# A second staging buffer and fewer GpSimd steps in a list-scheduled transformer block

## The chip, the cores and the metric

The kernel runs on one core of a Trainium2 chip. The metric is device time in microseconds (us) of one execution, lower is better. Before the change it took 759.53 us (median of three runs, 758.91 to 760.48); in the rounds that compare it with the changed kernel, 760.0 us (median of four, 758.91 to 761.48).

Short names, as the profile uses them: PE is TensorE, DVE is VectorE, ACT is ScalarE, POOL is GpSimd, SP is SyncE. L534 means line 534 of that kernel's source. An edit that adds lines shifts the numbers: L534 of before is L536 of after.

## The reference

One block with adaptive layernorm: linear attention, then a GEGLU feed-forward network.

```python
# S = 2048 rows, D = 1024, F = 3584, 32 heads; inputs bfloat16
mod = (silu(c) @ w_mod).reshape(..., 6, 1, -1)        # sa, ca, ga, sb, cb, gb
h = layernorm(x) * (1 + ca) + sa
x = x + ga * linear_attention(h, wqkv, wo)
h = layernorm(x) * (1 + cb) + sb                      # the second norm
x = x + gb * ((gelu(h @ w_gate) * (h @ w_up)) @ w_down)
```

## The kernel before

The kernel runs in stages: key/value/query, W_o, then twice (for two halves of the rows, g = 0 and 1) gate/up and down. Many matrix products use seven block products in place of eight, nested in places to a second level, so DVE makes many sums of blocks. Two jobs for later run behind the first gate/up stage:

- `wd_sums` makes second-level sums of W_down in seven steps: load rows, add on DVE, copy the result (768 KB) through a staging buffer `u` out to DRAM;
- `late_norm` normalises the second half's rows, in eight tiles.

```python
wdu_ring = Ring(199, [3, 4, HB], F16, 1)      # ONE staging buffer, 6 KB per partition

def wd_sums(c):
    raw, t, u, tt = wdr_ring(), wdt_ring(), wdu_ring(), wds_ring()
    # ... two loads (raw rows, first-level sums), ten sums on DVE into u and tt ...
    def last():
        tt_op(*steps[-1], ALU.add)
        gp.dma_start(out=u_scr[:, c], in_=u)                    # "us<-mem" in the profile
        for j in range(2):
            gp.dma_start(out=wd_full[f"t{2 * j + 1}"][:, rows, :], in_=tt[:, j])

def tile_norm(tl):                                              # in late_norm, cut
    sy.dma_start(out=xt, in_=x2_scr[b][r:r + P, :])
    ac.activation(out=junk, in_=xt, func=AF.Copy, accum_out=nmean)             # L1135
    gp.tensor_scalar(out=nmean, in0=nmean, scalar1=-1.0 / D, scalar2=None, op0=ALU.mult)  # L1136
    ac.activation(out=junk, in_=xt, func=AF.Square, bias=nmean, accum_out=ssq) # L1137
    gp.tensor_scalar(out=rstd, in0=ssq, scalar1=1.0 / D, scalar2=1e-5, op0=ALU.mult, op1=ALU.add)
    gp.tensor_tensor(out=rstd, in0=rstd, in1=nhalf, op=ALU.pow)
    gp.tensor_tensor(out=nb, in0=nmean, in1=rstd, op=ALU.mult)
    ac.activation(out=xh, in_=xt, func=AF.Identity, scale=rstd, bias=nb)
    gp.dma_start(out=xh_scr[g][b % 2][r:r + P, :], in_=xh)
```

Operations are not issued in the order written. The kernel has its own list scheduler: every call is recorded as an op with the memory it touches and a cost. PE's order is fixed; forward and backward sweeps decide the order on the other engines, and the best order by the model is issued. The cost model thus touches no data but moves instructions everywhere:

```python
elif op.eng == "POOL":
    op.cost = op.lat = 700 + n / 0.5          # ns; n = elements per partition
# ...
DMA_LATENCY, GBPS = 1500, 360                 # assumed: a DMA lands 1.5 us after its bytes at 360 GB/s

def issue(self):
    for op in self.order():                   # list schedule from op.cost, op.lat, dependencies
        self.calls[op.line](getattr(self.engines[op.eng], op.fn), op.args, op.kw)
```

These costs are what the scheduler assumes, not measurements.

Lines to know in the profile of before: L534 is the helper of all block sums on DVE; L781 copies a product from PSUM on ACT; L1284 and L1295 are first- and second-level matmuls of gate/up; L1338 is ACT seeding an accumulator; L1487 and L1531 are the down stage's matmuls.

Of the kernel before, what the change touches and what calls it, by code (L numbers as in the profile page):

```python
# [11 lines left out]
BF16 = mybir.dt.bfloat16  # L12
F16 = mybir.dt.float16
AF = mybir.ActivationFunctionType
ALU = mybir.AluOpType
# [8 lines left out]
class Plan:  # L24
# [98 lines left out]
    def cost(self, op, outs, ins):  # L123

        size = lambda a: math.prod(d[1] for d in a.ap[1:])
        n = max(size(a) for a in (outs if op.eng == "PE" else outs + ins))
        psum = any(a.tensor.name.startswith("psum") for a in outs + ins)
        wide = any(a.dtype == FP32 and size(a) > 8 for a in outs + ins)
        ptrs = sum(size(a) == 1 for a in ins)
        if op.eng == "PE":  # L130
            op.cost = n / 2.4 + 2.5
            op.lat = op.cost + 165
            if op.fn == "matmul" and outs[0].ap[0][1] <= 32:
                op.cost /= 3.5
        elif op.fn.startswith("dma"):
            a = outs[0]
            op.cost, op.bytes = 1000 if op.eng == "POOL" else 450, math.prod(d[1] for d in a.ap) * (4 if a.dtype == FP32 else 2)
            op.bytes *= 2 if "accum_op" in op.kw else 1
            op.load = a.tensor.name.startswith("mem")
            if op.fn == "dma_start_transpose":  # L140
                op.cost, op.bytes = self.transpose
            op.lat = op.cost
        elif op.eng == "ACT":
            op.cost = (55 if psum else 112) + n / 1.2 + 85 * ptrs
            op.lat = op.cost + 115
            f = op.kw.get("func")
            op.table = "g" if f == AF.Gelu_apprx_tanh else "e" if f in (AF.Exp, AF.Ln) else None
        elif op.eng == "POOL":
            op.cost = op.lat = 700 + n / 0.5
        else:  # L150
            rate = 1.0
            if op.fn in ("tensor_scalar", "tensor_scalar_mul", "tensor_scalar_add", "tensor_copy") and not wide:
                rate = 1.0 if psum else 4.0
            elif op.fn == "tensor_tensor" and not wide:
                rate = 2.0
            op.cost = 69 + n / (0.96 * rate) + 61 * ptrs
            op.lat = op.cost + 83
# [119 lines left out]
def kernel(  # L277
# [19 lines left out]
    S, D = x_in.shape  # L297
# [77 lines left out]
    def at(off, shape, dt):  # L375
        return Ring(off, shape, dt, 1)()
# [43 lines left out]
    HB = TG // 2  # L420
# [36 lines left out]
    rstd_ring = Ring(206.625, [1], FP32, 8)  # L457
    nb_ring = Ring(206.75, [1], FP32, 8)
    sum_ring = Ring(206.25, [1], FP32, 8)
# [25 lines left out]
    wds_ring = Ring(193, [2, 2, NW], F16, 1)  # L485
    wdt_ring = Ring(197, [2, NW], F16, 1)
    wdu_ring = Ring(199, [3, 4, HB], F16, 1)
    sub_a = [at(76 + 3.5 * j, [NPR // 2, HB], F16) for j in range(3)]
    sub_b = [at(189 + 3.5 * j, [NPR // 2, HB], F16) for j in range(4)]
    x2_ring = Ring(191, [D], BF16, 4)  # L490
    x2e_ring = Ring(144, [D], BF16, 3)
    xhe_ring = Ring(150, [D], F16, 3)
    junk = at(156, [D], F16)
    xh2_ring = Ring(199, [D], F16, 3)

    psT = Banks(0, 3)
# [23 lines left out]
    te, ve, ac, gp, sy = (plan.on(e) for e in ("PE", "DVE", "ACT", "POOL", "SP"))  # L520
# [605 lines left out]
    def late_norm(g):  # L1126


        def tile_norm(tl):
            b, r = 2 * g + tl // TT, tl % TT * P  # L1130
            xt, xh = x2e_ring(), xhe_ring()
            sy.dma_start(out=xt, in_=x2_scr[b][r:r + P, :])
            load = plan.ops[-1]
            nmean, ssq, rstd, nb = sum_ring(), sum_ring(), rstd_ring(), nb_ring()
            ac.activation(out=junk, in_=xt, func=AF.Copy, accum_out=nmean)  # L1135
            gp.tensor_scalar(out=nmean, in0=nmean, scalar1=-1.0 / D, scalar2=None, op0=ALU.mult)  # L1136
            ac.activation(out=junk, in_=xt, func=AF.Square, bias=nmean, accum_out=ssq)  # L1137
            gp.tensor_scalar(out=rstd, in0=ssq, scalar1=1.0 / D, scalar2=1e-5, op0=ALU.mult, op1=ALU.add)
            gp.tensor_tensor(out=rstd, in0=rstd, in1=nhalf, op=ALU.pow)
            gp.tensor_tensor(out=nb, in0=nmean, in1=rstd, op=ALU.mult)  # L1140
            ac.activation(out=xh, in_=xt, func=AF.Identity, scale=rstd, bias=nb)
            gp.dma_start(out=xh_scr[g][b % 2][r:r + P, :], in_=xh)
            return load

        return [lambda tl=tl: tile_norm(tl) for tl in range(2 * TT)]
# [573 lines left out]
```

## Time and profile before

| what | before |
|---|---|
| median of runs | 760.0 us |
| span of the profiled run | 757.8 us |
| busy: PE / DVE / ACT / POOL | 97% / 82% / 54% / 14% |
| granted TensorE clock | 1.0 |
| first gate/up stage (first matmul to first down matmul) | 173.8 us |
| second gate/up stage | 165.5 us |

The page of before: busy time of each engine, then PE's busy tenths and the granted clock, also in tenths, in 40 slices of the span.

```profile
span 757.8 us, 11401 instructions
## 1 busy us (share of the span) xinstructions
PE 735.8 (97%) x4164; PEld 391.6 (52%) x4164; DVE 622.7 (82%) x1288; ACT 412.2 (54%) x697; POOL 105.2 (14%) x199
...
PE   5999999999999999989999999999999999999997
...
PEclk9999999999999999999999999999999999999999
```

PE is full nearly everywhere (97% busy), so only a change that shortens PE's waits can win. How much is there? In the timeline, 40 matmuls of 512 columns start from 253.07 to 261.70 us: 0.216 us each. The first gate/up stage has 680 of these and 182 of 256 columns at 0.108 us, an estimate of 166.3 us; it takes 173.8, so it loses about 7.5 us.

PE's timeline of before in that stage, only lines with a wait of some size: start, length, engine, line, operation, operands, count, and in brackets PE's idle time ahead of it with its releaser.

```profile
326.22 1.02 PE L1284 MATMUL psum<-mem 128*128 128x512 f16 x4 [0.58 <-DVE mem L534]
327.75 0.38 PE L1295 MATMUL psum<-mem 128*128 128x256 f16 x2 [0.51 <-DVE psum L534]
331.62 0.38 PE L1295 MATMUL psum<-mem 128*128 128x256 f16 x2 [0.68 <-DVE psum L534]
338.61 1.02 PE L1284 MATMUL psum<-mem 128*128 128x512 f16 x4 [1.00 <-ACT mem L781]
377.13 1.02 PE L1284 MATMUL psum<-mem 128*128 128x512 f16 x4 [0.25 <-DVE mem L534]
378.67 0.38 PE L1295 MATMUL psum<-mem 128*128 128x256 f16 x2 [0.51 <-DVE psum L534]
382.13 0.38 PE L1295 MATMUL psum<-mem 128*128 128x256 f16 x2 [0.28 <-DVE psum L534]
```

There are three clusters: 326 to 332, 338.6, and 377 to 382 us. These gaps sum to less than the 7.5 us, because the view counts from a modelled end of the matmul before, about 0.16 us late (a 512-column matmul of L1284 lasts 379 ns in the page and the next starts after 216); smaller delays don't appear.

DVE's waits in the same stage (us in total, times, the longest), the DMA line of it:

```profile
DVE mem L534 <- DMA us<-mem: 4.9, 2, 3.0
```

DVE waited twice for a copy-out of its staging buffer. The chain of waits of before leads from the first one to PE (start, length, what):

```profile
310.91 8.86 DMA us<-mem
319.77 0.02 issue
319.79 2.37 DVE mem L534 x8
...
331.62 0.38 PE psum L1295 x2
...
335.17 1.65 POOL mem L1136
336.81 0.02 issue
336.84 1.24 ACT mem L1137 x2
338.08 0.49 ACT mem L781
338.57 0.04 issue
338.61 1.02 PE psum L1284 x4
```

A copy-out issued at 310.91 us lands 8.86 us later, and only then may the next step's sums fill the buffer; the first two gaps and the third follow from DVE being late. Then ACT stands between two passes of a late-norm tile for GpSimd's negate (L1136), which took 1.65 us here, and the copy that PE needs stands behind it in ACT's queue. Five of before's eight negates took 221 to 252 ns. What ran beside this one (the timeline of all engines from 333.6 to 336.9 us, two of its lines):

```profile
333.29 3.43 DVE L534 TENSOR_TENSOR mem<-mem 128x512 f16<-128x512 bf16 x10
335.17 1.64 POOL L1136 TENSOR_SCALAR mem<-mem 128x1 f32<-128x1 f32 x1
```

It ends (at 336.81 us) when a run of DVE sums with both operands in SBUF ends (336.72). The three long negates of before (1637, 1030 and 442 ns) lie beside such sums for 1550, 932 and 358 ns of their time, the five short ones for at most 84 ns. That is what the trace shows side by side.

The third cluster follows the other DVE wait, 1.9 us at 374 us: there the down stage's own sums overwrite the staging buffer, and the last copy-out is still under way.

### The profile page before, as it was taken

The numbers are of one execution on the slowest core, as the hardware profiler recorded it, in microseconds if no ns is written. First come the engines' busy times: TensorE is split into PE (matmuls) and PEld (weight loads), VectorE is DVE, ScalarE is ACT, GpSimd is POOL, SyncE is SP. The second block draws the span as 40 slices with busy tenths as digits, with TensorE's granted clock in tenths as the row PEclk, the third lists the DMA queues.
The fourth block names the chain that finished last, engine by engine and source line by source line (L and its number), as shares of the span: only waits on it lengthen the run. The fifth ranks groups of instructions, "written<-read, shape, count | busy, mean of one in ns | idle before, by whom it ended". The sixth has DMA issues, their size and how long they took to land.

```text
span 757.8 us, 11401 instructions
## 1 busy us (share of the span) xinstructions
PE 735.8 (97%) x4164; PEld 391.6 (52%) x4164; DVE 622.7 (82%) x1288; ACT 412.2 (54%) x697; POOL 105.2 (14%) x199
## 2 busy tenths in 40 slices
PE   5999999999999999989999999999999999999997
PEld 2454545443444445444445486645555555548664
DVE  7898986589897899899877779578889899897763
ACT  3674676668766578767565234016666666621000
POOL 1331433007121123141000001010000000000000
PEclk9999999999999999999999999999999999999999
DMA  9847067879389578875432999852323313399822
GB/s 313 304 119 253 27 154 165 299 286 178 100 242 312 210 263 289 281 261 211 135 103 52 290 275 280 290 185 84 112 65 102 112 56 112 101 273 294 281 100 74
DMA packets 140759, 144.78 MB, mean 191 GB/s; under 512 B 33440, under 2 KB 120864, under 8 KB 139936
## 3 DMA queue, kind: packets, MB, share of 16 engines
q1 hardware_dynamic: 124016, 106.31, 46.0%
q0 software_dynamic: 14336, 35.66, 15.1%
q10 hardware_dynamic: 2352, 2.10, 0.8%
q8 instruction: 32, 0.52, 0.3%
q14 instruction: 23, 0.19, 0.1%
HBM read 111.81 MB, written 32.24 MB: 190 GB/s over the span
## 4 chain that ended last, share of the span: by engine, by line
PE 76%; DVE 7%; ACT 5%; DMA 5%; issue 4%; POOL 1%; SPq 1%; POOLq 0%; DVEq 0%; ACTq 0%
PE psum L1284 25%; PE psum L1487 13%; PE psum L1531 8%; PE psum L836 6%; PE psum L1295 6%; PE psum L1176 6%; DVE mem L534 5%; PE psum L906 4%; PE psum L935 4%; DMA us<-mem 2%; DMA mem<-in_A_wqkv_dram 2%; DMA mem<-in_w_mod_dram 1%; PE psum L950 1%; PE psum L962 1%; DVE mem L975 1%
## 5 line engine op out<-in xcount | busy, mean ns | idle before, releaser
L534 DVE TENSOR_TENSOR mem<-mem 128x512 f16<-128x512 f16 (+11 forms) x633 | 292.0, 506 | 15.1 <-DMA us<-mem 4.9
L1284 PE MATMUL psum<-mem 128*128 128x512 f16 x1248 | 299.3, 379 | 2.8 <-ACT mem L781 1.0
L534 DVE TENSOR_TENSOR mem<-psum,mem 128x512 f16<-128x512 f32 (+4 forms) x260 | 192.3, 748 | 70.7 <-ACT mem L781 25.8
L781 ACT ACTIVATE mem<-psum 128x256 f32<-128x256 f32 (+2 forms) x228 | 123.2, 554 | 119.2 <-PE psum L1284 43.2
L1284 PEld LDWEIGHTS <-mem 128*128 128x128 f16 (+1 forms) x1248 | 122.1, 98 | 114.4 <-issue 5.2
L1487 PE MATMUL psum<-mem 128*128 128x512 f16 (+2 forms) x462 | 99.2, 373 | 0.5 <-DVE mem L534 0.5
L1295 PE MATMUL psum<-mem 128*128 128x256 f16 x560 | 89.5, 272 | 2.4 <-DVE psum L534 2.2
L1295 PEld LDWEIGHTS <-mem 128*128 128x128 f16 (+1 forms) x560 | 54.7, 98 | 48.1 <-issue 6.5
L1487 PEld LDWEIGHTS <-mem 128*128 128x128 f16 x462 | 45.2, 98 | 49.9 <-issue 0.7
L1338 ACT ACTIVATE psum<-psum 128x512 f32<-128x512 f32 x56 | 32.9, 587 | 62.1 <-PE psum L1284 31.5
L1531 PE MATMUL psum<-mem 128*128 128x256 f16 (+1 forms) x588 | 66.2, 273 | 0.0
L836 PE MATMUL psum<-mem 128*128 128x512 f16 (+1 forms) x280 | 62.5, 379 | 0.0
L1531 PEld LDWEIGHTS <-mem 128*128 128x128 f16 x588 | 57.5, 98 | 9.2
L1176 PE MATMUL psum<-mem 128*128 128x512 f16 x256 | 57.4, 379 | 0.7 <-DVE mem L534 0.7
L906 PE MATMUL psum<-mem 128*128 128x512 f16 x224 | 51.1, 379 | 0.1
L534 DVE TENSOR_TENSOR psum<-psum,mem 128x256 f32<-128x256 f32 x80 | 34.1, 426 | 11.5 <-ACT mem L781 11.5
L836 PEld LDWEIGHTS <-mem 128*128 128x128 f16 x280 | 27.0, 98 | 31.2
L1355 ACT ACTIVATE mem<-psum 128x512 f16<-128x512 f32 x56 | 33.3, 596 | 17.4 <-PE psum L1284 17.1
L1176 PEld LDWEIGHTS <-mem 128*128 128x128 bf16 x256 | 25.1, 98 | 31.0 <-issue 0.9
L906 PEld LDWEIGHTS <-mem 128*128 128x128 f16 (+1 forms) x224 | 21.4, 97 | 26.9 <-issue 2.1
L1365 ACT ACTIVATE mem<-mem 128x512 f16<-128x512 f16 x56 | 34.9, 629 | 0.5 <-DVE mem L534 0.3
L612 DVE BATCH_NORM_STATS2 mem<-mem 128x6 f32<-128x512 bf16 x48 | 30.9, 677 | 1.5 <-DMA mem<-in_A_x_dram 1.5
(127 smaller groups left out, 564.8 us busy)
## 6 DMA issues: line engine op xcount, KB each, us to landing
mem<-in_B_w_gate_dram SPq DMA_DIRECT2D x14, 1024.0 KB, 5.2
mem<-in_B_w_up_dram SPq DMA_DIRECT2D x14, 1024.0 KB, 5.7
mem<-in_w_mod_dram SPq DMA_DIRECT2D x24, 512.0 KB, 6.7
mem<-us SPq DMA_DIRECT2D x24, 448.0 KB, 7.8
mem<-in_A_x_dram SPq DMA_DIRECT2D x32, 256.0 KB, 3.9
ts<-in_B_w_down_dram POOLq DMA_DIRECT2D x28, 256.0 KB, 7.2
us<-mem POOLq DMA_DIRECT2D x7, 768.0 KB, 7.4
mem<-in_B_w_down_dram SPq DMA_DIRECT2D x12, 448.0 KB, 7.1
```

Of the source, the lines that this page charges most:

```text
L534: ve.tensor_tensor(out=out, in0=a, in1=b, op=op)
L781: ac.activation(out=t, in_=ps, func=AF.Copy)
L836: te.matmul(ps, lhsT=A[:, k, i * P:(i + 1) * P], rhs=B[:, k, :], start=(start and k == 0), stop=(k == KH - 1), skip_group_check=True)
L906: te.matmul(o, lhsT=W[:, k, (j0 + i) * P:(j0 + i + 1) * P], rhs=h_form(a, k), start=(start and k == 0), stop=(k == KH - 1), skip_group_che ...
L1176: te.matmul(psw[:, half, :], lhsT=pqT[b][:, g, tl * P:(tl + 1) * P], rhs=Wp[:, g, half * NW:(half + 1) * NW], start=(g == 0), stop=(g == K ...
L1284: te.matmul(ps, lhsT=a[:, k, e, :], rhs=b[:, k, :], start=(start and k == 0), stop=(k == KH - 1), skip_group_check=True)
L1295: te.matmul(ps, lhsT=self.x[a][:, k, :], rhs=self.y[y][:, k, :], start=(start and k == 0), stop=(k == KH // 2 - 1), skip_group_check=True)
L1338: ac.activation(out=z, in_=x, func=AF.Copy)
L1355: ac.activation(out=o, in_=ps, func=AF.Gelu_apprx_tanh)
L1365: ac.activation(out=o, in_=o, func=AF.Gelu_apprx_tanh)
L1487: te.matmul(psm[:, q, c], lhsT=A[:, i, q * P:(q + 1) * P], rhs=wt[:, i, c], start=(start and i == 0), stop=(i == NPR - 1), skip_group_chec ...
L1531: te.matmul(ps[:, q, :], lhsT=a[:, k, q * P:(q + 1) * P], rhs=y[:, k, :], start=(start and q == 0 and k == 0), stop=(k == NPR // 2 - 1), s ...
```

## The change

The intent: the late norm gives most of its 128x1 operations to DVE and loses one (the negate folds into a scale on the ACT pass); the staging buffer gets a twin; and the scheduler is told that a small GpSimd operation costs less time but a longer latency. The diff is complete:

```diff
         elif op.eng == "POOL":
-            op.cost = op.lat = 700 + n / 0.5
+            op.cost = 500 if n <= 8 else 250 + n / 0.46
+            op.lat = 1800 if n <= 8 else op.cost
@@
     wdu_ring = Ring(199, [3, 4, HB], F16, 1)
+    wdu_ring.slots += Ring(183, [3, 4, HB], F16, 1).slots
@@
-    junk = at(156, [D], F16)
+    junk = at(156, [D], BF16)
@@
-            nmean, ssq, rstd, nb = sum_ring(), sum_ring(), rstd_ring(), nb_ring()
-            ac.activation(out=junk, in_=xt, func=AF.Copy, accum_out=nmean)
-            gp.tensor_scalar(out=nmean, in0=nmean, scalar1=-1.0 / D, scalar2=None, op0=ALU.mult)
-            ac.activation(out=junk, in_=xt, func=AF.Square, bias=nmean, accum_out=ssq)
-            gp.tensor_scalar(out=rstd, in0=ssq, scalar1=1.0 / D, scalar2=1e-5, op0=ALU.mult, op1=ALU.add)
+            nmean, var, rstd, nb = sum_ring(), sum_ring(), rstd_ring(), nb_ring()
+            root = D ** -0.5
+            ac.activation(out=junk, in_=xt, func=AF.Copy, scale=-root / D, accum_out=nmean)
+            ac.activation(out=junk, in_=xt, func=AF.Square, scale=root, bias=nmean, accum_out=var)
+            ve.tensor_scalar_add(out=rstd, in0=var, scalar1=1e-5)
             gp.tensor_tensor(out=rstd, in0=rstd, in1=nhalf, op=ALU.pow)
-            gp.tensor_tensor(out=nb, in0=nmean, in1=rstd, op=ALU.mult)
+            ve.tensor_scalar(out=nb, in0=nmean, scalar1=rstd, scalar2=1.0 / root, op0=ALU.mult, op1=ALU.mult)
             ac.activation(out=xh, in_=xt, func=AF.Identity, scale=rstd, bias=nb)
```

So the change has three named parts, called here cost, slot and norm, and a fourth thing that none of its lines says: the order that the scheduler makes from them. A comparison of the two instruction streams shows PE's order the same, and other orders on DVE, ACT, POOL and SP.

## The prediction

> **What bounds the kernel.** The page of before: PE is busy 97% of a 757.8 us span, DVE 82%, ACT 54%, POOL 14%; granted clock 1.0. Gaps in the PE timeline: about 8.7 us at the start, some 3.5 us from 174 to 239 us, and 4.5 us in the first gate/up stage (253 to 427 us). That stage lasts 174 us; its 680 matmuls of 512 columns at 0.216 us and 182 of 256 columns at 0.108 us need about 166 us (estimate from the trace's pitch), so it loses nearly 8 us; the second gate/up stage loses about 2.
>
> In the first stage DVE is nearly full (5.8 to 6.0 us of most 6 us slices). The chain of waits shows two places where it is late: the copy-out of the W_down second-level sums, issued at 310.9 us, lands at 319.8 us, and DVE idles 2.97 us for its single buffer; PE then loses 0.58, 0.51 and 0.68 us. A later copy-out (issued 365.75, landed 374.3) costs DVE 1.9 us and PE about 1.0 us. A third loss, 1.00 us at 338.6 us, goes through the late norm: ACT waits 1.27 us for POOL's negate, which took 1.64 us instead of its usual 0.22 us.
>
> **What the change does.** Matmul order is identical. (1) The Copy-to-Square round trip through POOL is gone (0.53 us mean plus handoff, per tile). Sixteen 128x1 operations are new on DVE: one of 128x8 takes 0.157 us, some 0.1 us of pitch, so 1.6 to 2.6 us of DVE work, where DVE is full. POOL had time for its 8 us. [...]
> (2) The second staging buffer removes the wait at 316.8 us: reuse is then two sums (about 25 us) away, against 8.9 us to land. The 374 us wait stays: there the down stage's sums overwrite the first buffer, and the new order keeps about the same distance (some 13 DVE operations).
> (3) The scheduler's new GpSimd cost reorders DVE, ACT and POOL, in the first 180 us too, where PE has hardly a gap: nothing to win, a little to lose.
>
> **Sum.** Won: 1.8 us (staging wait) + 1.0 us (POOL round trip) + up to 1 us of small seed waits; with less behind it, perhaps 2 more. Given back: 1 to 2 us by added DVE work and by DVE[...] now itself waiting for ACT's sums and POOL's power (three late tiles are bunched, and the down stage's differences wait for their last ACT passes). Net -2 to -4 us.
>
> Predicted 756.5 us; 8 times in 10 within 752.5 to 760. Chances: faster by over 2% 0.01, within 2% 0.97, slower 0.02.
>
> **What would show it.** The 2.97 us DVE wait near 317 us is gone, and PE's gaps at 326 to 332 us with it; the one near 374 us remains; ACT no longer waits for POOL before Square; the first gate/up stage is 2 to 4 us shorter than 174 us, the others equal within 1 us; sixteen DVE operations of 0.15 us appear.
>
> **What would make it wrong.** DVE blocked on POOL's power behind DMA issues, or on ACT in the bunched tail, for several us; other single buffers (raw rows, first-level sums, their copy-outs) taking over the wait; the reordered first third opening PE gaps; or all of the loss freed, up to 6 us.

The sum: its net of -2 to -4 us on the 759.53 us of before gives 755.5 to 757.5, and 756.5 is the middle.

## The result, and the profile after

The changed kernel is correct and takes 756.72 us (median of four runs, 755.78 to 758.08) against 760.0 us: a ratio of 0.9957, 95% interval 0.9933 to 0.9981. A ratio here is the mean time of one kernel's fast runs over that of the other's of the same rounds, so not quite the ratio of the medians.

Stage by stage, from the first matmul of each stage in the profiled runs:

| stage | before | after | difference |
|---|---|---|---|
| up to W_o (keys, values, queries) | 192.3 | 192.9 | +0.6 |
| W_o | 60.8 | 60.8 | 0.0 |
| first gate/up | 173.8 | 171.0 | -2.9 |
| first down | 80.4 | 80.4 | 0.0 |
| second gate/up | 165.5 | 164.9 | -0.6 |
| second down, end | 85.0 | 85.0 | 0.0 |

The same lines of the page of after (without the heading):

```profile
span 754.9 us, 11379 instructions
PE 734.4 (97%) x4144; PEld 391.3 (52%) x4164; DVE 623.4 (83%) x1304; ACT 411.6 (55%) x697; POOL 95.8 (13%) x175
```

Twenty-four small operations left POOL (199 to 175) and sixteen came to DVE (1288 to 1304); the other eight are gone. (PE's 4144 for 4164 is matmul records missing from the trace, since the weight loads are 4164 in both.)

All of PE's waits in the first gate/up stage of after:

```profile
294.79 4.48 PE L1286 MATMUL psum<-mem 128*128 128x512 f16 x20 [0.33 <-ACT psum L1340]
312.29 1.02 PE L1286 MATMUL psum<-mem 128*128 128x512 f16 x4 [0.21 <-ACT mem L783]
319.95 4.48 PE L1286 MATMUL psum<-mem 128*128 128x512 f16 x20 [0.19 <-ACT psum L1340]
```

All three clusters are gone in this profile, the one near 377 too, which the prediction expected to stay. DVE's waits in the stage, all lines of 1 us or more but those on PE and on the copies of L783:

```profile
DVE mem L1140 <- ACT mem L1139: 2.5, 2, 1.5
...
DVE mem L536 <- DMA mem<-ts: 2.0, 1, 2.0
...
DVE mem L536 <- DMA mem<-in_B_w_down_dram: 1.0, 1, 1.0
```

No wait for `us<-mem` is left. In its place DVE now waits 3.0 us for two loads of the sums' inputs, and 2.5 us for ACT's Square pass ahead of the new epsilon addition (L1140). None of these reaches PE as a gap of more than 0.33 us in this profile. The sixteen new DVE operations, by line (duration min/median/max in ns):

```profile
L1140 DVE TENSOR_SCALAR mem<-mem x8: 143/151/154, 267.0 to 347.9; 128x1 f32<-128x1 f32 x8
```

```profile
L1142 DVE TENSOR_SCALAR mem<-mem x8: 203/206/208, 268.6 to 368.5; 128x1 f32<-128x1 f32 x8
```

They are 8 x 0.151 + 8 x 0.206 = 2.9 us of DVE time. Where DVE has nothing to wait for, the next operation starts 0.06 to 0.20 us after the start of one of them ("some 0.1 us of pitch" in the prediction). The addition, L1140, has an immediate operand; L1142 multiplies by a [128, 1] operand and an immediate.

Nothing here yet says which part did what, since order, slot, norm and cost changed at once.

### The profile page after: what moved, and what is told of

Its sections match the earlier page's. It is cut to its first block, busy times and chain, and to the rows that moved or that the text cites. A ratio compares the mean times of both kernels' runs of the same rounds, so it can differ in the third digit from the quotient of the medians.

```text
span 754.9 us, 11379 instructions
## 1 busy us (share of the span) xinstructions
PE 734.4 (97%) x4144; PEld 391.3 (52%) x4164; DVE 623.4 (83%) x1304; ACT 411.6 (55%) x697; POOL 95.8 (13%) x175
## 4 chain that ended last, share of the span: by engine, by line
PE 80%; DVE 8%; ACT 6%; DMA 4%; issue 1%; SPq 1%; DVEq 0%; ACTq 0%
PE psum L1286 28%; PE psum L1489 13%; PE psum L1533 9%; PE psum L1297 7%; DVE mem L536 7%; PE psum L838 6%; PE psum L1178 6%; PE psum L908 4%; PE psum L937 4%; DMA mem<-in_A_wqkv_dram 2%; DMA mem<-in_B_w_up_dram 1%; DMA mem<-in_w_mod_dram 1%; PE psum L952 1%; ACT psum L965 1%; ACT mem L967 1%
## 5 line engine op out<-in xcount | busy, mean ns | idle before, releaser
L536 DVE TENSOR_TENSOR mem<-psum,mem 128x512 f16<-128x512 f32 (+4 forms) x260 | 192.3, 748 | 67.5 <-ACT mem L783 22.6
L783 ACT ACTIVATE mem<-psum 128x256 f32<-128x256 f32 (+2 forms) x228 | 123.2, 555 | 121.1 <-PE psum L1533 46.4
```

Source lines behind the costliest of these rows:

```text
L536: ve.tensor_tensor(out=out, in0=a, in1=b, op=op)
L783: ac.activation(out=t, in_=ps, func=AF.Copy)
```

## The experiments

Three explanations stood against each other:

1. **Buffer.** The second buffer removes the staging wait, whatever the order.
2. **Negate.** The round trip through POOL goes, whatever the order. Its rival: moving the other sixteen operations off POOL matters, or costs.
3. **Order.** The new cost and dependencies give a different schedule, and that is the gain (or hides a loss).

Two kinds of kernel tell them apart. A *pinned* kernel (names that begin with p) changes one thing physically while the scheduler still plans with the old memory or engine, so that the instruction order of before, or of after, is kept; that the order was the same on every engine was checked by comparing the streams. A *free* kernel (names that begin with e, except the held one) has some of the three parts as they stand in the diff, and the scheduler does what it likes: s is slot, n is norm, c is cost. All kernels were timed in five rounds beside before; the medians of before in the three sets of rounds were 758.85, 759.48 and 759.62 us. A run over 1.5% above the fastest of its kernel counts as slow and is left out of the ratios; medians and ranges are of all runs. The texts were written before each run, and have short names of their own for the theories.

### Pinned: after once more

No edit. The question is the spread of the effect itself.

> The changed kernel itself, on the same chip as the three pinned kernels beside it: 0.9957 of before again (0.994 to 0.998). The first gate/up stage about 171.0 us against 174.0, the stages before it together 0.5 to 1 us longer than in before.

Measured: 757.87 us against 758.85, ratio 0.9981 (0.9968 to 0.9995); first gate/up stage 171.75 us. The gain is there again but smaller, and the two intervals overlap. So the gain is 0.2 to 0.4%, and a stage length from a single profile is good to about 0.8 us (170.96 and 171.75 for the same kernel). The two profiles differ by one PE gap, near the old third cluster:

```profile
381.30 0.38 PE L1297 MATMUL psum<-mem 128*128 128x256 f16 x2 [0.83 <-DVE psum L536]
```

Just before it DVE waits 1.10 us for a load of W_up at 378.9 us; in the first profile that wait is 0.34 us and PE has no gap. The stage up to W_o took 193.7 us here, 0.8 more than in the first profile; the granted clock is 0.62 from 16 to 20 us in this one and 1.00 in the other.

### Pinned: before's order, two staging buffers

Physically the second buffer; while recording a `wd_sums` step the scheduler is told that the second slot's addresses are the first's.

```diff
+    wdu_ring.slots += Ring(183, [3, 4, HB], F16, 1).slots
@@ in the recorder of memory cells
+            if self.staging is not None and name.startswith("mem"):
+                got = {u + 16 * 64 if 183 * 64 <= u < 189 * 64 else u for u in got}
@@ around each sum and copy-out of wd_sums
+            plan.staging = c % 2
             tt_op(*steps[-1], ALU.add)
             gp.dma_start(out=u_scr[:, c], in_=u)
+            plan.staging = None
```

> Before's instruction order on every engine, word for word, but the second-level sums really use two staging buffers. Theory A (the staging wait was on the path): DVE's 2.97 us wait near 317 us and PE's gaps of 0.58, 0.51 and 0.68 us after it go, the wait near 374 us stays (there the down stage overwrites the first buffer), and the time falls by 1.5 to 2.5 us, ratio 0.9967 to 0.998. Rival B (the gain comes from the new order): within 0.5 us of before, ratio 0.9993 to 1.0007.

Measured: 759.23 us, ratio 0.9999 (0.9987 to 1.0012); first gate/up stage 172.55 us, 1.3 less than before. PE's later waits in that stage (0.2 us ones left out):

```profile
330.41 0.38 PE L1306 MATMUL psum<-mem 128*128 128x256 f16 x2 [0.48 <-DVE psum L538]
337.41 1.02 PE L1295 MATMUL psum<-mem 128*128 128x512 f16 x4 [1.00 <-ACT mem L785]
376.26 1.02 PE L1295 MATMUL psum<-mem 128*128 128x512 f16 x4 [0.57 <-DVE mem L538]
377.79 0.38 PE L1306 MATMUL psum<-mem 128*128 128x256 f16 x2 [0.51 <-DVE psum L538]
381.26 0.38 PE L1306 MATMUL psum<-mem 128*128 128x256 f16 x2 [0.28 <-DVE psum L538]
```

DVE's waits for copy-outs in the stage:

```profile
DVE mem L538 <- DMA us<-mem: 2.2, 1, 2.2
```

Of two waits for the copy-out one is left. The gaps of 0.58 and 0.51 us near 326 are gone and the 0.68 near 331 became 0.48: 1.3 us. The POOL gap of 1.00 us and the cluster near 377 stay (its first gap is 0.57 us in place of 0.25). So in the profile the buffer does what it is for. Its worth, 1 us in 759, is at the edge of what the timing resolves: the interval reaches down only to -0.13%, and the median shows nothing. The ratio lies where the text put the rival, not theory A (0.9967 to 0.998): the buffer's effect is shown by the waits of one profile, not by the time.

### Pinned: before's order, two buffers and no negate

As above, plus the negate folded into the Copy's scale (and the junk tile in bfloat16, as in the change); the recorded POOL operation keeps its place in the plan and is skipped at issue.

```diff
-            ac.activation(out=junk, in_=xt, func=AF.Copy, accum_out=nmean)
+            ac.activation(out=junk, in_=xt, func=AF.Copy, scale=-1.0 / D, accum_out=nmean)
             gp.tensor_scalar(out=nmean, in0=nmean, scalar1=-1.0 / D, scalar2=None, op0=ALU.mult)
+            plan.dropped.add(len(plan.ops) - 1)
```

> Before's order on every engine, with two staging buffers and without GpSimd's negate (its factor goes into ScalarE's Copy); the other small operations stay on GpSimd. Theory A: the 1.00 us gap at 337 us that the two-buffer kernel still had goes, the first gate/up stage takes 171.2 to 172.0 us against 172.55 with two buffers alone and 173.83 in before, the other stages as in before; ratio 0.9965 to 0.9985. Rival (the negate was not on the path): 172.4 us or more.

Measured: 758.12 us against 759.62, ratio 0.9978 (0.9965 to 0.9991); stage 171.61 us, another 0.9 less. PE's waits from 330 us on (two more, of 0.51 and 0.28 us, follow the last line):

```profile
331.58 0.38 PE L1309 MATMUL psum<-mem 128*128 128x256 f16 x2 [0.25 <-DVE psum L540]
340.96 0.38 PE L1309 MATMUL psum<-mem 128*128 128x256 f16 x2 [0.35 <-DVE psum L540]
376.69 1.02 PE L1298 MATMUL psum<-mem 128*128 128x512 f16 x4 [0.48 <-DVE mem L540]
```

The 1.00 us gap is gone, and a DVE gap of 0.35 us took some of its place. Against the 7.5 us that before loses in this stage (length less 166.3), the kernels lose 6.2 with the buffer, 5.3 with buffer and no negate, and 4.7 in after. The two mechanisms account for 2.2 us of the 2.9 that after won in the stage; the remaining 0.65 is within the spread of one profile. This kernel, with before's order, is about as fast as after. Time and stage length are as theory A expected. What it keeps is the cluster near 377, which is gone in the profiles with after's order but for the single gap of 0.83 us above.

### Pinned: after's order, one staging buffer

The slot line taken out of after, while the scheduler still plans with two.

> After's instruction order on every engine, but one staging buffer in fact. Theory A: DVE waits for copy-outs come back, more than before's since this order counts on two buffers; 2 to 4 us over after, so about before's time or a little more (ratio to before 0.998 to 1.002). Rival B (the order alone makes the gain): within 0.7 us of after, ratio 0.995 to 0.9965.

Measured: 778.45 us, ratio 1.0253 (1.0239 to 1.0267), first gate/up stage 193.5 us, with PE gaps of 5.69, 2.81, 2.57 and 3.83 us. That is some 20 us over after, where theory A expected 2 to 4 and its rival none. The result was wrong (relative error 0.052), which was not intended: in one place, the second step, after's order writes its first sum into the buffer (at 291.3 us) before the copy-out of the first step is issued (at 292.0), which is right only with two buffers. So this is not a clean price of the buffer: one buffer is not a legal memory for that order. What it does show is that after's order leans on the second buffer: DVE waits 19.3 us for copy-outs in four places, three of them (13.3 us) in steps where the order is legal.

### Pinned: after's order, the sixteen operations back on GpSimd

```diff
-                self.calls[op.line](getattr(self.engines[op.eng], op.fn), op.args, op.kw)
+                eng = "POOL" if op.n in self.late else op.eng      # late: the 16 small ones
+                self.calls[op.line](getattr(self.engines[eng], op.fn), op.args, op.kw)
```

> After's order, but the sixteen 128x1 operations of the late norm that moved to VectorE are issued on GpSimd at the same places. Theory A (the move off GpSimd pays only by taking the negate from between the two ScalarE passes; on VectorE the rest costs 1 to 2 us of a full engine): 0 to 1.5 us faster than after. Rival C (moving them off GpSimd is itself a gain[...]): 0.7 us or more slower than after.

Measured: 756.95 us, ratio 0.9971 (0.9959 to 0.9984), stage 170.89 us. That is after, within the spread (0.9 us below its second measurement; the rival needed 0.7 us above). Moving these operations to VectorE neither won nor cost anything that can be measured here (stage 170.96 and 171.75 us with them on VectorE): what helped was to drop the negate between two ACT passes (0.9 us, pinned), not to move the rest.

### Free: each part alone

Each is before with the lines of that part of the diff and no others.

> Before plus the second staging buffer alone; the scheduler is free to use it. Theory A (buffer and shorter norm chain each take their own waits away): first gate/up stage 171.5 to 172.7 us (before 173.8; pinned order gave 172.55), no DVE wait for the copy-out near 317 us, the gap of about 1 us behind GpSimd's negate still there; ratio 0.9975 to 0.999. Rival D (only the new GpSimd cost line, through the order, makes the gain): 173.3 us or more, ratio 0.9993 or more.

Slot alone: 758.71 us, ratio 0.9987 (0.9975 to 0.9999), first gate/up stage 173.3 us. DVE waits for no copy-out in that stage, but 3.2 us for loads of W_up; the time is as theory A expected, the stage is not.

> Before plus the late norm's new operations alone (one buffer, old GpSimd cost of 702 ns in the scheduler). Theory A: the 1.0 us gap behind the negate goes, the waits for the single staging buffer stay: first gate/up stage 172 to 174 us, ratio 0.998 to 1.0005. Rival D: 173.3 us or more. Rival E (the norm move is the whole gain): 171.5 us or less.

Norm alone (with the bfloat16 junk): 784.0 us, six runs of 769.88 to 792.16, three of them slow; ratio of the fast ones 1.0298 (1.0251 to 1.0346). First gate/up 177.4, first down stage 88.7 us in place of 80.4.

> Before with the scheduler's new GpSimd cost line alone; same operations and buffers. Theory A: first gate/up stage within 0.7 us of 173.8, what comes before the first gate/up stage 0.2 to 1 us longer than in before (253.1 us), ratio 0.9995 to 1.0015. Rival D: first gate/up stage 172.3 us or less, ratio 0.998 or less.

Cost alone: 764.05 us, ratio 1.0057 (1.0044 to 1.0069), first gate/up 176.5 us. So rival D, by which the cost line alone makes the gain, is out.

So two of the three parts, alone, make the kernel slower, norm by 3%, a loss that no text gave, and although the pinned runs show norm's negate to be a gain. For cost, which touches no data, that can only be the schedule; for norm it is inferred, since the pinned runs changed the same operations without a loss.

### Free: pairs of parts

> The change without the scheduler's new cost line. Theory A: first gate/up stage 170.5 to 172 us as in after (171.0 and 171.8), and without the reordering of the first third, so as fast as after or up to 0.7 us faster; ratio 0.9955 to 0.998. Rival D: 173 us or more, ratio 0.999 or more.

Slot and norm: 775.61 us (768.19 to 800.15, one slow run), ratio 1.0187 (1.0141 to 1.0234), where theory A expected a gain.

> Buffer and new cost line, old norm. Read beforehand from the order alone: on ScalarE, three scalings of the second half of the next stage's activations stand before two copies of the first down stage that PE needs (after has none before them). Theory F (that order is what cost the kernels with the new norm and without the cost line 8 us in the first down stage): the first down stage takes 86 us or more instead of 80.4, PE waits once for ScalarE over 4 us, and the ratio is 1.008 or more. Rival G (the norm on VectorE without the cost line is the cause): first down stage 80.4 us, ratio under 1.003.

Cost and slot: 776.59 us (767.1 to 788.92, three slow), ratio 1.0114 (1.0092 to 1.0135). Theory F was right here: 91.3 us in the first down stage, with a PE wait of 9.02 us for ACT.

> New norm and new cost line, one buffer. From the order alone: no scaling of the second half stands before the two copies. Theory F: first down stage 80.4 us; the waits for the single staging buffer stay, first gate/up stage 172 to 176 us; ratio 0.998 to 1.004. Rival G (or any rule by which the new norm alone slows the down stage): 86 us or more, ratio over 1.008.

Cost and norm: 772.94 us (769.84 to 775.82), ratio 1.0166 (1.0143 to 1.019).

| parts | none | s | c | n | sn | cs | cn | all (after) |
|---|---|---|---|---|---|---|---|---|
| ratio | 1 | 0.999 | 1.006 | 1.030 | 1.019 | 1.011 | 1.017 | 0.996, 0.998 |
| first gate/up, us | 173.8 | 173.3 | 176.5 | 177.4 | 176.3 | 176.2 | 181.6 | 171.0, 171.8 |
| first down, us | 80.4 | 80.4 | 80.4 | 88.7 | 89.3 | 91.3 | 86.5 | 80.4 |

The parts don't add. Each set gives another order. Five of the six smaller sets lose 0.6 to 3%; slot alone may gain a little (its interval ends at 0.9999, and it overlaps that of after's second measurement); only the full set was measured twice, and both intervals end below 1 (0.9981 and 0.9995). The stage lengths are of one profile each, and runs of one kernel spread: that of norm is its fastest run, that of cost and norm its slowest. Two places lose. In the first gate/up stage DVE now stands for loads of W_up (7.9 us in the norm kernel, 5.7 in slot and norm; 0.3 and 1.1 in the profiles of after). And in the first down stage, where no part of the change has any work, PE stops once for 4 to 9 us. PE's only wait in that stage with slot and norm:

```profile
466.61 3.14 PE L1532 MATMUL psum<-mem 128*128 128x256 f16 x14 [6.30 <-ACT mem L782]
```

ACT's timeline of that kernel just before (L782 copies products that PE needs, L1157 scales the second half's normalised rows, which come through a transposing load `mem<-xhs`):

```profile
453.19 1.51 ACT L1157 ACTIVATE mem<-mem 128x512 f16<-128x512 f16 x2
463.85 2.22 ACT L1157 ACTIVATE mem<-mem 128x512 f16<-128x512 f16 x3 [9.15 <-DMA mem<-xhs]
465.98 0.57 ACT L782 ACTIVATE mem<-psum 128x512 f32<-128x512 f32 x1
```

The scheduler put three scalings, whose data come by a DMA, ahead of the copy that PE needs. ACT ran them in that order: it stood 9.15 us before the scalings, until the DMA had landed, and started the copy only behind them, at 465.98 us, although PE's last product before its stall was done at 460.31 us. The price is more than the stall: in the four kernels the stage is 1.7 to 2.5 us longer than its stall explains. Windows of slot and norm, from us to us: length, busy time and count of PE, its weight loads, DVE, ACT and POOL, then granted clock, DMA share, GB/s.

```profile
462.00:466.00 4.00, 0.00 (x0) 0.00 (x0) 1.74 (x2) 2.15 (x4) 0.00 (x0) 0.83 1.03 343
466.00:470.00 4.00, 3.40 (x16) 2.19 (x16) 0.00 (x0) 2.88 (x6) 0.00 (x0) 0.50 1.16 286
```

The granted clock is 0.50 for the 4 us after the stall. With each of these stalls it drops: to 0.50 after 9.02 us with cost and slot (465 to 470 us), to 0.66 after 4.17 us with cost and norm (470 to 475 us); for norm alone, after 6.59 us, the page shows 8 tenths in the slice from 461 to 480 us. After one of 1.01 us (next run) it stays 1.00. But shorter stalls than these did it too. In the first gate/up stage of cost and norm PE stopped for 1.49 us at 358.0 and for 0.51 us at 360.5; the same view of it:

```profile
358.00:361.00 3.00, 1.05 (x5) 0.38 (x4) 3.00 (x8) 1.01 (x2) 0.54 (x1) 1.00 0.57 141
361.00:365.00 4.00, 3.94 (x13) 1.71 (x13) 3.38 (x9) 0.97 (x2) 0.00 (x0) 0.57 0.62 222
```

In the kernel with cost alone, gaps of 1.65 and 1.79 us left it at 1.00 (its mean over the whole span is 1.0), and so did 5.56 us of idle at the start of before, from 2.3 to 7.9 us (1.00 in every window from 0 to 20 us). So how much idle time it takes is not settled here.

### The same order with the scalings held back

Slot and norm, its plan taken, and only the second-half scalings (with what depends on them) that stood before the last two of those copies moved to just after them.

```diff
-            for op in self.order():
+            for op in self.held(self.order()):     # moves the marked scalings behind the last copies
```

> New norm and two buffers without the cost line, as in the run that took 89.3 us in the first down stage, with one change after the planning: the six second-half scalings that stood before the two copies (and nothing else) stand right after them. Theory F: first down stage 80.4 to 81.5 us, PE's wait of over 6 us for ScalarE gone, 8 us or more faster than that run, ratio 0.999 to 1.006, and no wide spread of times. Rival: the stall moves elsewhere, first down stage over 84 us.

Measured: in the profiled run PE's stall of 6.30 us is gone; this is its only wait left in that stage, the clock stays 1.00 in that stage, and the stage takes 81.9 us in place of 89.3 (80.4 to 81.5 expected):

```profile
460.39 3.18 PE L1504 MATMUL psum<-mem 128*128 128x512 f16 x14 [1.01 <-DMA mem<-ts]
```

So, in this one profile, the order of ACT's instructions made that stall. But the timed runs say that it is not all, and miss the expected ratio of 0.999 to 1.006: 771.62 us, six runs of 761.99 to 776.85, three slow; ratio of the fast ones 1.0095 (1.0057 to 1.0132). The profiled execution was the fastest of them. And the pair cost and norm, whose ACT order is good, was expected by the same theory to be well in that stage and was not: PE stopped 4.17 us for a 1792 KB load of first-level sums (`mem<-ts`), which landed 16.1 us after its issue.

What these kernels seem to share was looked for and not tested: in the good ones (before, after, slot, cost) that 1792 KB load is issued between 1.1 us before and 0.05 us after the second transposing load, and lands in 8.8 to 11.3 us; in the five bad ones it is issued 0.6 to 4.0 us after it and lands in 10.6 to 19.1 us. In two of these (slot and norm, cost and slot) there are slices in which the DMA engines are 90% busy or more yet move only about 30 GB/s (290 in slices near them); in the other three the slow slices show DMA engines that are mostly or in part idle. Why, and why four of these five spread by 2 to 4% from run to run (before: 0.4%), stays open.

## Why the prediction was right or wrong

**The total: right.** Predicted 756.5, measured 756.72 us. The second measurement gave 757.87, also within the range; but its gain (ratio 0.9981, 1.4 us) is under the net 2 to 4 us of the sum, and the range up to 760 holds the medians of before too (758.85 to 760.0). So the total is a weak test, and what counts is the parts.

**First staging wait and gaps at 326 to 332 us gone: right.** The pinned run with two buffers shows that the buffer alone removes this wait of DVE and two of PE's three gaps; the third fell from 0.68 to 0.48 us. The term "1.8 us (staging wait)" measured 1.3 us in the stage of one profile, and not visibly in the timing.

**POOL round trip gone, 1.0 us: right.** Pinned, 0.9 us. The term "up to 1 us of small seed waits" was not won: PE's waits for ACT's seeds (L1338) sum to 0.66 us in before and 0.52 in after.

**"The 374 us wait stays": wrong.** The step that failed is "the new order keeps about the same distance (some 13 DVE operations)". The traces show that the distance was not the same. In before the last copy-out is issued at 365.75 us and its buffer is wanted at 372.4, 6.6 us and 11 DVE operations later. In after it is issued at 384.53 and wanted at 396.4, 11.9 us and 23 operations later; DVE works without a break in both stretches. And this copy-out landed in 3.6 us in place of 8.5. By these figures either change would have been enough to end the wait. The pinned runs keep before's order and keep the wait (2.2 us with two buffers): the new order removed it, and the buffer alone didn't.

**"Given back: 1 to 2 us by added DVE work": not shown.** Sixteen operations came with 2.9 us of DVE time, and DVE waits for ACT and for new loads as predicted, but the same order with those operations on POOL has the same stage length (170.89 against 170.96 and 171.75). So this term was sized too large. It rested on DVE being "nearly full"; DVE is busy for 148.6 of the stage's 173.8 us in before, and only 12 of 29 slices of 6 us hold 5.8 us or more. That it and the forgotten 374 us gain have opposite signs is part of why the total came out so near.

**Other stages equal within 1 us: right,** with -0.6 us in the second gate/up stage, where no part has work: all three kernels with before's order show 165.5 and all four with after's order 164.9, an effect of order. The first 180 us were expected to lose "a little"; they show +0.6, but three kernels of one and the same order spread from 192.3 to 194.0 us there, so that is not shown. The record shows where much of the spread comes from: in the two longest of the seven profiles with before's or after's order (194.0 and 193.7 us, one of each) the granted clock is about 0.6 from 16 to 20 us, in the other five 1.00 (192.3 and 192.7 with before's order, 192.5 to 192.9 with after's).

**What the prediction did not see.** It treated the three parts as a sum of terms. That holds only with the order pinned. With the scheduler free the parts alone or in pairs lost up to 3%, and nothing in the prediction said so: it argued from the parts, and only the comparison of the whole streams was about the order that was in fact run.

**What stays open.** Of the 2.9 us in the first gate/up stage 0.65 us is not assigned; the slow loads in the first down stage of the five kernels named above are not explained. Whether the longer distance or the quicker landing ended DVE's wait before the third cluster was not varied. No version was found that is clearly faster than after: before's order with buffer and without the negate, and after with its operations on POOL, equal it within the spread.

## What to carry to other kernels

When a kernel orders its own instructions by a cost model, test one edit with the order pinned: here the edits' own effects were about 1 us each, and with the reorderings they set off the kernels ranged from a gain of 0.4% to a loss of 3%. Remove a round trip that stands between two passes of one engine (here 0.9 us of the stage) before moving small operations off an engine with time to spare (POOL, 14% busy: nothing measurable here), and judge a buffer's reuse by the microseconds between issue and next use against the landing time, both in the order that will run: here a change of order took them from 6.6 against 8.5 to 11.9 against 3.6. Avoid placing work that waits for a DMA ahead of a copy that the bottleneck needs on the same engine: three kernels here that had it stalled for 6.3 to 9.0 us. The granted clock dropped with these stalls and with one of 4.2 us (to 0.50 and 0.66 where it was read over 4 or 5 us), and the stage was 1.7 to 2.5 us longer than the stall alone.
